# Turning y of three chunks on VectorE and in transfers of 128-byte pieces instead of on TensorE

## The chip, the core and the metric

The kernel runs on one core of a Trainium2 chip. The core has TensorE (PE; its weight loads are listed apart as PEld), VectorE (DVE), ScalarE (ACT), GpSimd (POOL) and SyncE (SP), which here issues every transfer between HBM and the on-chip memory (SBUF). Each of them works through its own instructions strictly in order. PSUM is the small memory that TensorE writes. Sixteen DMA engines carry the transfers. The metric is the time of one execution on the device, in microseconds (us).

## The reference, cut to what matters

```python
x  = A_x                                             # 2048 tokens x 512
xn = layernorm(x)
s  = attention(xn, A_wqkv) @ A_wo                    # 32 heads of 16, a window of 256 keys
y  = layernorm(xn)                                   # what this change is about
h  = gelu(y @ B_w1 + B_b1)                           # 1792 columns
g  = silu(h @ B_w2 + B_b2)
return x + s * g
```

A matmul contracts over the 128 partitions of its operands. y is made with tokens on the partitions (a layernorm is a sum along a row), and `y @ B_w1` needs it with the 512 model columns on the partitions: four blocks `kt` of 128 columns by 512 tokens. Getting from the one to the other is what "turning" means below. Products are taken in a split form: a tile is cut into a rounded high part (by ACT) and the rest (by DVE), and three matmuls stand for one (`PASSES`, line 67; `split`, line 69).

## The kernel before, in words

The first 430 us or so are attention, which the change does not touch. Then comes the MLP, over four chunks of 512 tokens. Chunk 0's y was turned earlier, during attention (`y_turn`).

**The loops (lines 1060 to 1155).** For c = 0 and 1 a loop runs over i = 0 to 14. At each i, `activate` (line 1070) takes the hidden product `h` of column block f through Gelu on ACT into `g` and cuts it into `gh` (ACT) and `gl` (DVE); `project` (line 919) adds the block before into four `acc` banks with twelve matmuls; `hidden` (line 1065) makes the product `h` of the block after next with twelve matmuls, into one of two banks. For c = 0 nearly all hidden products were made during attention, so the loop there is a row of `project` blocks. Then `end_chunk` (line 929) adds b2 (DVE), takes Silu (ACT, `gated`), and for each of four token blocks i calls `between(i)`, makes `s`, the attention's output projection (twelve matmuls, two banks in turn), multiplies it into `gated` (DVE), adds x (POOL, `xo`) and stores.

**Chunks 2 and 3** are computed together after these loops by a recursive scheme with seven products, whose inputs are y of chunk 2, y of chunk 3 and sums and differences of their blocks (`t1` to `t4`). They are prepared inside the loop of c = 1.

**Where y is turned, before.** Chunk 1: `between(0)` and `between(2)` of c = 0 call `y_transpose` (line 642): for each block, four TensorE transposes into a PSUM bank `yt`, then `split` into `mlp["yy"]`, the input of the hidden products of c = 1. Chunk 2: `first_y` (line 996) at i = 3 and 4 of c = 1. Chunk 3: `second_y` (line 1002) at i = 8 and 10, with two steps `more` and `most` called at i = 9, 11 and 12 (line 1089). `transposed` (line 986) issues the four transposes of a block. y of chunks 2 and 3 is loaded from x and normalised twice (`steps2`, line 1051): statistics on DVE, a power on POOL, the scaling on ACT.

**What sets the order.** On PE, DVE, ACT and POOL the order is that of the program text, so everything behind a waiting instruction waits too. SP's order in this part is set by a scheduler (line 855); once set it is also strict. SP's transfers take turns on eight completion counters, so one transfer is issued only when the eighth before it has landed.

**Other transfers that matter here.** `load_o` (line 893) fetches attention output `or` and a broadcast reciprocal `w` (from `rden_d`); both are 256 KB in eight groups of sixteen rows. The y tiles of chunks 1 to 3 share four buffers (`yp`, line 867): a tile of the next chunk can be loaded only when the last reader of the old one is done. Small tiles, `g`, `or` and `xo` among them, share five buffers (`t2`, line 58).

Of the kernel before, what the change touches and what calls it, by code (L numbers as in the profile page):

```python
# [9 lines left out]
F32 = mybir.dt.float32  # L10
# [8 lines left out]
P = 128  # L19
NCH = S // 512  # L20
NKB = S // P
KT = D // P
# [28 lines left out]
def mixer_kernel(ctx, tc, x, wqk, wv, wo, w1, b1, w2, b2, out):  # L51


    nc = SimpleNamespace(**{name: Ordered(tc, name) for name in ("tensor", "vector", "scalar", "gpsimd", "sync")})
# [3 lines left out]
    t2 = ctx.enter_context(tc.tile_pool(name="t2", bufs=5))  # L58
    small = ctx.enter_context(tc.tile_pool(name="small", bufs=3))
    dram = ctx.enter_context(tc.tile_pool(name="dram", bufs=1, space=bass.MemoryType.DRAM))  # L60
# [8 lines left out]
    def split(dst_hi, dst_lo, src, eng=None):  # L69

        (eng or nc.scalar.copy)(dst_hi, src)
        nc.vector.tensor_sub(dst_lo, src, dst_hi.bitcast(F32))
# [87 lines left out]
    def run(steps):  # L160
        for step in steps:
            step()
# [13 lines left out]
    def open_slot(i):  # L176
# [9 lines left out]
    w_d = {"w1": dram.tile([P, NF * 512], F32, name="w1_d"), "w2": dram.tile([P, NF * 512], F32, name="w2_d"),  # L186
           "wo": dram.tile([P, 4 * 512], F32, name="wo_d")}
    g_d = dram.tile([NF, P, 512], F32, name="g_d")
    mT_d = dram.tile([NQ, NCH, 32, P], F32, name="mT_d")


# [31 lines left out]
    ident = const.tile([P, P], F32, name="ident")  # L223
# [360 lines left out]
    mlp = {}  # L584
# [54 lines left out]
    def y_steps(a, b):  # L639
        run(mlp["ln"][a:b])  # L640

    def y_transpose(c, kt, ps=None):
        ts = mlp["y"]
        if ps is None:
            ps = ps_yt.tile([P, 512], F32, tag="b", name=f"yt_{c}_{kt}")
        for i in range(4):
            nc.tensor.transpose(ps[:, P * i: P * (i + 1)], ts[i][:, P * kt: P * (kt + 1)], ident)
        split(mlp["yy"][0][kt], mlp["yy"][1][kt], ps)

    def hidden_mm(ps, f, k):  # L650
        kt, (a, b) = k // 3, PASSES[k % 3]
        nc.tensor.matmul(ps, w1_part(a, f)[:, P * kt: P * (kt + 1)], mlp["yy"][b][kt],
                         start=(k == 0), stop=(k == 3 * KT - 1))
# [209 lines left out]
    ps_yt = ctx.enter_context(tc.tile_pool(name="ps_yt", bufs=2, space=PSUM))  # L863
# [9 lines left out]
    for f in range(6, NF, 2):  # L873
        t = gp.tile([P, 2, 512], F32, tag="ohl", name=f"hr_{f}", bufs=4)
# [7 lines left out]
    def load_y(c):  # L882
        if c > 1:
            return load_x(c, ((mlp["yp"], "y"),), "y")
        return [load(mlp["yp"], "y", xn_d[4 * c + i], f"y_{c}_{i}") for i in range(4)]

    def fetch_sums():
        den = t2.tile([P, 512], F32, tag="t2", name="den")
        for g in range(4):
            nc.sync.dma_start(den[32 * g: 32 * g + 32], oT_d[g, :, DH].rearrange("a (c t) -> a c t", c=NCH))  # L890
        return den
# [84 lines left out]
    kept = {}  # L976
# [6 lines left out]
        first = 256 * (j % (2 if j < 4 else 4))  # L983
        return at[:, first: first + 256 * n]

    def transposed(c, kt):
        ps = ps_yt.tile([P, 512], F32, tag="b", name=f"yt_{c}_{kt}")
        for i in range(4):
            nc.tensor.transpose(ps[:, P * i: P * (i + 1)], mlp["y"][i][:, P * kt: P * (kt + 1)], ident)
        return ps  # L990

    def put(name, kt, src):

        split(inputs(name, kt, 0), inputs(name, kt, 1), src)

    def first_y(kt):

        ps = transposed(2, kt)
        nc.scalar.copy(kept[kt // 2][:, kt % 2], ps)
        put("21" if kt > 1 else "11", kt % 2, ps)  # L1000

    def second_y(kt):

        t1, t4 = kept[0][:, kt], kept[1][:, kt]
        t3, t2_ = (t2.tile([P, 512], F32, tag="t2", name=f"yt{k}_{kt}") for k in (3, 2))
        ps = transposed(3, kt)
        nc.vector.tensor_sub(t1, ps, t1)
        nc.scalar.copy(t3, ps)
        ps = transposed(3, kt + 2)
        nc.vector.tensor_sub(t2_, ps, t1)  # L1010
        nc.vector.tensor_sub(t3, ps, t3)

        def more():
            put("22", kt, ps)
            nc.vector.tensor_sub(t4, t4, t2_)
            put("t1", kt, t1)
            put("t3", kt, t3)

        def most():
            put("t2", kt, t2_)  # L1020
            put("t4", kt, t4)
        return more, most

# [36 lines left out]
    for c in range(2):  # L1060
        accs = open_accs(c)
        gs, os_, hs, wanted = {}, [], {}, []
        made = ready if c == 0 else {}

        def hidden(f):
            hs[f] = ps_st.tile([P, 512], F32, tag="b", name=f"h_{c}_{f}")
            for k in range(3 * KT):
                hidden_mm(hs[f], f, k)

        def activate(f):  # L1070
            if f in made and f in soon:
                gs[f] = made[f]
                return
            src = made[f] if f in made else hs.pop(f)
            g = src if f in made and f < 2 else t2.tile([P, 512], F32, tag="t2", name=f"g_{c}_{f}")
            nc.scalar.activation(g, src, AF.Gelu_apprx_tanh, bias=b1s[:, f: f + 1])
            gs[f] = split_g(c, f, g, nc.scalar.copy)

        order = [2, 3, 0, 1, 4, 5, *range(6, NF)] if c == 0 else [*range(NF)]
        if c:  # L1080
            hidden(0)
            hidden(1)
        o_from, o_late = (0, 0) if c else (8, 1)
        for i in range(NF + 1):
            if i < NF:
                activate(order[i])
            if c and i in (1, 2, 6, 7):
                y_steps(6, 10)
            if c and i in (9, 11):
                rest[0]()  # L1090
            if c and i in (9, 12):
                rest[1]()
            if c and i == 14:
                kept["w"] = bigp.tile([P, 768], F32R, tag="wb1", name="wsh")
                combine_w(0)
            if c == 0:
                for kind, f in late_w[LATE[i]: LATE[i + 1]]:
                    settle(kind, f, nc.scalar.copy, nc.vector)
            if i >= 1:
                project(accs, [(order[i - 1], gs.pop(order[i - 1]))], order[0], order[-1])  # L1100
            if i + 2 < NF and order[i + 2] not in made and order[i + 2] > 1:
                hidden(order[i + 2])
            if c == 0:
                if i == 2:
                    den = fetch_sums()
                if 4 <= i < 8:
                    nc.vector.reciprocal(den[:, P * (i - 4): P * (i - 3)], den[:, P * (i - 4): P * (i - 3)])
                    if i == 7:
                        nc.sync.dma_start(rden_d.rearrange("g a (c t) -> (g a c) t", c=NCH), den)
                if i == 4:  # L1110
                    mlp["y"] = load_y(1)
                if i == 6:
                    mlp["ln"] = layernorm(mlp["y"], "C1", False)
                for back, (a, b) in enumerate(((0, 2), (2, 4), (4, 5), (5, 6), (6, 8), (8, 10))):
                    if i == 6 + min(back, 5):
                        y_steps(a, b)
            else:
                steps2(i)
                if i == 3:
                    kept[0] = gated[:, 2:4]  # L1120
                    first_y(0)
                    first_y(1)
                if i == 4:
                    kept[1] = bigp.tile([P, 2, 512], F32, tag="wb1", name="y2_21")
                    first_y(2)
                    first_y(3)
                    mlp["y"] = load_y(3)
                if i in (8, 10):
                    rest = second_y(i // 10)
                if i == 12:  # L1130
                    fetch_pair(0)
            k = i - o_from
            if 0 <= k - 2 - o_late < 4:
                os_.append(split_o(c, k - 2 - o_late, wanted[k - 2 - o_late][0]))
            if 0 <= k - 1 - o_late < 4:
                nc.vector.tensor_mul(wanted[k - 1 - o_late][0], *wanted[k - 1 - o_late])
            if 0 <= k < 4:
                wanted.append(load_o(c, k))
            if c and i in (0, 1, 5, 6):
                y_steps(5, 6)  # L1140
        if c == 0:
            gated = bigp.tile([P, 4, 512], F32, tag="wa", name="gated")

        def between(i):
            if c == 0 and i in (0, 2):
                y_transpose(1, i)
                y_transpose(1, i + 1)
                if i == 2:
                    mlp["y"] = load_y(2)
            if c == 1 and i in (1, 2):  # L1150
                split_w(0, 2 * i - 2)
                split_w(0, 2 * i - 1)
        end_chunk(c, accs, os_, between)
        if c == 0:
            steps2(-1)
# [148 lines left out]
```

## Time and profile before

| what | us |
|---|---|
| median of 3 runs | 750.75 (750.43 to 750.79) |
| the profiled execution | 750.88 |
| its span, first to last instruction | 749.2 |
| PE busy in the span | 733.9 |
| DVE, ACT, POOL busy | 511.7, 441.1, 299.3 |
| the granted clock of TensorE, mean of the span | 1.0 |

All numbers below come from one profiled execution. Its span is 1.7 us shorter than its own time; the rest lies around the first and the last instruction. Because helper functions issue all instructions, every row names line 43, and rows are told apart by the tiles they write and read (`out<-in`). A bracket at the end of a row of the timeline says how long the engine had been idle and what ended it. In the view of stretches each engine has its busy time and in brackets its count of instructions; then come the granted clock, the mean busy share of the sixteen DMA engines, and GB/s.

### The profile page before, as it was taken

The page shows a single profiled execution, that of the slowest core. Times are in us where ns is not written, and L with a number is a line of the kernel's source. Part 1 is how long each engine was busy: PE and PEld are TensorE (multiplying, and loading weights), DVE is VectorE, ACT ScalarE, POOL GpSimd, SP SyncE. Part 2 cuts the span into 40 slices and gives each one's busy share as a digit, 9 for nine tenths or more (in the row PEclk, how much of TensorE's full clock was granted, in tenths as well). Part 3 has the DMA queues.
Part 4 walks back from the last instruction along what each step waited for, and adds up shares of the span by engine and source line. Part 5 has one row for each costly group of instructions (what it writes and reads, how often), then busy time and mean ns, then how long its engine had stood idle before and what let it go on. Part 6 is the DMA issues. An engine that isn't in the chain of part 4 may idle for free.

```text
span 749.2 us, 18758 instructions
## 1 busy us (share of the span) xinstructions
PE 733.9 (98%) x7408; PEld 590.4 (79%) x7408; DVE 511.7 (68%) x781; ACT 441.1 (59%) x746; POOL 299.3 (40%) x644
## 2 busy tenths in 40 slices
PE   8999999999999999999999999999999999999997
PEld 7886777777778888777776788888888888888886
DVE  7886777877766778887872648763576765676743
ACT  7757767867667676778877745444463744442001
POOL 7413757767666555767877600120102000001102
PEclk9999999999999999999999999999999999999999
DMA  8633356766555535647724482542012232253611
GB/s 288 191 74 78 84 133 149 201 168 183 152 142 145 144 90 142 162 111 190 200 86 148 133 286 94 165 151 82 31 45 102 93 100 72 70 174 123 222 45 56
DMA packets 56951, 99.40 MB, mean 133 GB/s; under 512 B 11104, under 2 KB 11360, under 8 KB 56864
## 3 DMA queue, kind: packets, MB, share of 16 engines
q1 hardware_dynamic: 56864, 98.21, 45.7%
q8 instruction: 58, 0.95, 0.5%
q14 instruction: 29, 0.24, 0.1%
HBM read 51.39 MB, written 29.62 MB: 108 GB/s over the span
## 4 chain that ended last, share of the span: by engine, by line
PE 89%; ACT 5%; DVE 2%; POOL 2%; issue 1%; DMA 1%; SPq 0%; DVEq 0%; ACTq 0%; POOLq 0%
PE acc L43 20%; PE fb L43 18%; PE zo L43 11%; PE stb L43 9%; PE p L43 9%; PE s L43 6%; PE h L43 6%; PE xy L43 5%; ACT pt L43 4%; PE pv L43 3%; POOL pt L43 1%; DVE xy L43 1%; PE yt L43 1%; DMA x<-in_x_dram 1%; DVE mt L43 0%
## 5 line engine op out<-in xcount | busy, mean ns | idle before, releaser
L43 POOL TENSOR_SCALAR_AFFINE_SELECT pt<-pt 128x256 f32<-128x256 f32 x480 | 193.8, 428 | 132.9 <-ACT pt L43 131.7
L43 ACT ACTIVATE pt<-stb 128x768 f32<-128x768 f32 (+1 forms) x244 | 188.8, 774 | 62.4 <-PE stb L43 54.8
L43 DVE TENSOR_REDUCE mt<-xy 128x4 f32<-128x1024 f32 (+1 forms) x128 | 152.6, 1192 | 4.4
L43 DVE COPY_PREDICATED xy<-upper,zo 128x512 f32<-128x512 int32 x112 | 77.8, 695 | 70.6 <-PE xy L43 63.1
L43 POOL TENSOR_TENSOR xo<-xo,gated 128x512 f32<-128x512 f32 x15 | 20.3, 1358 | 216.8 <-DVE gated L43 192.9
L43 PE MATMUL fb<-xnT,wqb 64*128 64x512 f32 (+1 forms) x684 | 104.8, 397 | 0.3
L43 PE MATMUL zo<-pt,vt 128*17 128x128 f32 x2880 | 103.7, 275 | 0.3 <-POOL pt L43 0.3
L43 PE MATMUL stb<-qk 64*128 64x384 f32 (+1 forms) x488 | 97.2, 393 | 6.2 <-ACT pt L43 4.1
L43 PE MATMUL acc<-w,gh 128*128 128x512 f32 x320 | 98.9, 390 | 0.0
L43 PEld LDWEIGHTS stb<-qk 64*128 64x128 f32 x488 | 45.8, 183 | 51.6 <-ACT pt L43 46.6
L43 PEld LDWEIGHTS zo<-pt,vt 128*17 128x17 f32 x2880 | 67.5, 97 | 15.6 <-issue 6.3
L43 PEld LDWEIGHTS fb<-xnT,wqb 64*128 64x128 f32 (+1 forms) x684 | 64.7, 185 | 11.0 <-DVE pjr L43 1.4
L43 PEld LDWEIGHTS acc<-w,gh 128*128 128x128 f32 x320 | 59.8, 188 | 12.3
L43 PE MATMUL acc<-w,gl 128*128 128x512 f32 x160 | 62.4, 390 | 0.0
L43 PE MATMUL xy<-qk 64*128 64x256 f32 (+2 forms) x536 | 58.4, 291 | 0.2 <-DVE mt L43 0.2
L43 PEld LDWEIGHTS xy<-qk 64*128 64x128 f32 x536 | 46.7, 185 | 6.7 <-issue 3.1
L43 ACT COPY oraw<-zo 128x128 f32<-128x128 f32 x128 | 34.2, 267 | 29.2 <-PE zo L43 28.9
L43 ACT ACTIVATE gated<-acc 128x512 f32<-128x512 f32 x16 | 8.7, 596 | 65.6 <-DVE acc L43 65.6
L43 PE MATMUL s<-wos,ohl 128*128 128x512 f32 (+1 forms) x204 | 44.7, 378 | 0.0
L43 PEld LDWEIGHTS s<-wos,ohl 128*128 128x128 f32 x204 | 36.7, 188 | 7.2 <-DVE gated L43 0.2
L43 PEld LDWEIGHTS zo<-qk 64*128 64x128 f32 x448 | 38.5, 185 | 4.4 <-issue 1.4
L43 ACT COPY p<-p 128x512 f32<-128x512 f32 x21 | 12.3, 586 | 49.7 <-PE p L43 42.3
(195 smaller groups left out, 1241.5 us busy)
## 6 DMA issues: line engine op xcount, KB each, us to landing
qk<-sh SPq DMA_DIRECT2D x128, 128.0 KB
qk<-pjr SPq DMA_DIRECT2D x64, 128.0 KB
oT_d<-oraw SPq DMA_DIRECT2D x32, 256.0 KB
w_d<-in_w_dram SPq DMA_DIRECT2D x14, 512.0 KB
x<-in_x_dram SPq DMA_DIRECT2D x16, 256.0 KB
or<-oT_d SPq DMA_DIRECT2D x16, 256.0 KB
w<-rden_d SPq DMA_DIRECT2D x16, 256.0 KB
xo<-in_x_dram SPq DMA_DIRECT2D x16, 256.0 KB
```

The source lines that it names most:

```text
L43: r = issue(*args, **kwargs)
```

## The change

For chunks 1, 2 and 3 the TensorE transposes go away. `turn_y` has DVE transpose a tile of y (128 tokens x 512) in place, each square of 32 x 32 on its own, and stores the tile to a scratch tensor `z_d` in HBM. `fetch_y` then puts one block `kt` in place with four transfers of 64 KB: each writes 32 partitions, sixteen pieces of 128 bytes per partition, 512 pieces in all. So a chunk has four DVE transposes, four stores and sixteen fetches.

Chunk 1 is turned at i = 11 and 12 of c = 0 and fetched at i = 13 straight into the low halves of `mlp["yy"]`; `settle_y`, in `between(0)` and `between(2)`, makes the split there. Chunk 2 is turned at i = 3 of c = 1, fetched at i = 4 and split by `first_y` at i = 5 and 6. Chunk 3 is turned at i = 8, fetched by halves at i = 8 and 10, used by `second_y` at i = 9 and 11, with `more` and `most` at i = 10, 12 and 13. The loads of the next chunk's y move with the fetches.

```diff
+    z_d = dram.tile([NCH, 4, P, 512], F32, name="z_d")
...
-    def y_transpose(c, kt, ps=None):
-        ts = mlp["y"]
-        if ps is None:
-            ps = ps_yt.tile([P, 512], F32, tag="b", name=f"yt_{c}_{kt}")
-        for i in range(4):
-            nc.tensor.transpose(ps[:, P * i: P * (i + 1)], ts[i][:, P * kt: P * (kt + 1)], ident)
-        split(mlp["yy"][0][kt], mlp["yy"][1][kt], ps)
...
+    def turn_y(c, i):
+
+        y = mlp["y"][i]
+        nc.vector.transpose(y, y)
+        nc.sync.dma_start(z_d[c, i], y)
+
+    def fetch_y(c, kt, dst):
+
+        for k in range(4):
+            at = z_d[c, 0, 0, 128 * kt + 32 * k: 128 * kt + 32 * k + 32]
+            nc.sync.dma_start(dst[32 * k: 32 * k + 32].rearrange("p (t j) -> p t j", j=32),
+                              bass.AP(tensor=at.tensor, offset=at.offset, ap=[[512, 32], [32 * 512, 16], [1, 32]]))
+
+    def settle_y(kt):
+
+        hi, lo = mlp["yy"][0][kt], mlp["yy"][1][kt]
+        split(hi, lo, lo.bitcast(F32))
...
-    def transposed(c, kt):
-        ps = ps_yt.tile([P, 512], F32, tag="b", name=f"yt_{c}_{kt}")
-        for i in range(4):
-            nc.tensor.transpose(ps[:, P * i: P * (i + 1)], mlp["y"][i][:, P * kt: P * (kt + 1)], ident)
-        return ps
...
     def first_y(kt):
 
-        ps = transposed(2, kt)
-        nc.scalar.copy(kept[kt // 2][:, kt % 2], ps)
-        put("21" if kt > 1 else "11", kt % 2, ps)
+        put("21" if kt > 1 else "11", kt % 2, kept[kt // 2][:, kt % 2])
+
+    def fetch_second(kt):
+
+        kept["y3"] = [t2.tile([P, 512], F32, tag="t2", name=f"y3_{k}") for k in (kt, kt + 2)]
+        for k, t in enumerate(kept["y3"]):
+            fetch_y(3, kt + 2 * k, t)
 
     def second_y(kt):
 
         t1, t4 = kept[0][:, kt], kept[1][:, kt]
-        t3, t2_ = (t2.tile([P, 512], F32, tag="t2", name=f"yt{k}_{kt}") for k in (3, 2))
-        ps = transposed(3, kt)
-        nc.vector.tensor_sub(t1, ps, t1)
-        nc.scalar.copy(t3, ps)
-        ps = transposed(3, kt + 2)
-        nc.vector.tensor_sub(t2_, ps, t1)
-        nc.vector.tensor_sub(t3, ps, t3)
+        one, two = kept["y3"]
+        nc.vector.tensor_sub(t1, one, t1)
+        nc.vector.tensor_sub(one, two, one)
 
         def more():
-            put("22", kt, ps)
-            nc.vector.tensor_sub(t4, t4, t2_)
+            put("22", kt, two)
             put("t1", kt, t1)
-            put("t3", kt, t3)
+            put("t3", kt, one)
 
         def most():
-            put("t2", kt, t2_)
+            nc.vector.tensor_sub(two, two, t1)
+            put("t2", kt, two)
+            nc.vector.tensor_sub(t4, t4, two)
             put("t4", kt, t4)
         return more, most
...
-            if c and i in (9, 11):
+            if c and i in (10, 12):
                 rest[0]()
-            if c and i in (9, 12):
+            if c and i in (10, 13):
                 rest[1]()
...
+                if i in (11, 12):
+                    turn_y(1, 2 * i - 22)
+                    turn_y(1, 2 * i - 21)
+                if i == 13:
+                    for kt in range(KT):
+                        fetch_y(1, kt, mlp["yy"][1][kt].bitcast(F32))
+                    mlp["y"] = load_y(2)
             else:
                 steps2(i)
                 if i == 3:
+                    for k in range(4):
+                        turn_y(2, k)
+                if i == 4:
                     kept[0] = gated[:, 2:4]
-                    first_y(0)
-                    first_y(1)
-                if i == 4:
                     kept[1] = bigp.tile([P, 2, 512], F32, tag="wb1", name="y2_21")
-                    first_y(2)
-                    first_y(3)
+                    for kt in range(KT):
+                        fetch_y(2, kt, kept[kt // 2][:, kt % 2])
                     mlp["y"] = load_y(3)
-                if i in (8, 10):
-                    rest = second_y(i // 10)
+                if i in (5, 6):
+                    first_y(2 * i - 10)
+                    first_y(2 * i - 9)
+                if i == 8:
+                    for k in range(4):
+                        turn_y(3, k)
+                    fetch_second(0)
+                if i in (9, 11):
+                    rest = second_y(i // 11)
+                if i == 10:
+                    fetch_second(1)
...
         def between(i):
             if c == 0 and i in (0, 2):
-                y_transpose(1, i)
-                y_transpose(1, i + 1)
-                if i == 2:
-                    mlp["y"] = load_y(2)
+                settle_y(i)
+                settle_y(i + 1)
```

## The prediction

> **What bounds the kernel now.** First the page, then the chain of work that ended last, cut to the end of chunk 0 and the loop of c = 1.
>
> ```profile
> span 749.2 us, 18758 instructions
> PE 733.9 (98%) x7408; PEld 590.4 (79%) x7408; DVE 511.7 (68%) x781; ACT 441.1 (59%) x746; POOL 299.3 (40%) x644
> ```
>
> ```profile
> 446.16 30.12 PE acc L43 x132
> 476.27 0.87 PE yt L43 x8
> 477.15 5.46 PE s L43 x24
> 482.61 0.87 PE yt L43 x8
> 483.48 5.68 PE s L43 x24
> 489.16 8.16 PE h L43 x36
> ...
> 510.92 2.72 PE h L43 x12
> ...
> 554.48 0.88 PE yt L43 x8
> ```
>
> TensorE is never idle here: each piece begins where the one before ends. Twelve matmuls take 2.72 us. The transposes stand on the chain in six groups of eight, 0.87 us each, two at the end of chunk 0 and four in the loop of c = 1. What is taken off PE is won, and what makes PE wait is lost.
>
> What will supply y instead is SP's queue, so its timeline comes next, with the first load of the kernel and a row from attention (64 KB and more into 32 partitions, three-level pattern).
>
> ```profile
> 0.79 1.81 SPq L43 DMA_DIRECT2D x<-in_x_dram  x4
> ...
> 191.68 2.54 SPq L43 DMA_DIRECT2D qk<-sh  x4
> ...
> 457.91 0.32 SPq L43 DMA_DIRECT2D rden_d<-den  x1
> 458.28 0.62 SPq L43 DMA_DIRECT2D or<-oT_d  x1
> 459.88 1.20 SPq L43 DMA_DIRECT2D w<-rden_d  x2
> 461.13 0.57 SPq L43 DMA_DIRECT2D or<-oT_d  x1
> 461.75 1.48 SPq L43 DMA_DIRECT2D w<-rden_d  x2
> 463.90 1.08 SPq L43 DMA_DIRECT2D or<-oT_d  x1
> 466.69 3.76 SPq L43 DMA_DIRECT2D w<-rden_d  x2
> ```
>
> ```profile
> 3.57 0.69 DVE L43 BATCH_NORM_STATS2 bnA<-x 128x6 f32<-128x512 f32 x1 [0.68 <-DMA x<-in_x_dram]
> ...
> 467.18 1.00 DVE L43 TENSOR_SCALAR y<-y,mvC,rsC 128x512 f32<-128x512 f32 x2
> 469.76 0.68 DVE L43 TENSOR_TENSOR gl<-g,gh 128x512 fp32r<-128x512 f32 x1
> 472.03 0.69 DVE L43 TENSOR_TENSOR gl<-g,gh 128x512 fp32r<-128x512 f32 x1
> 475.28 0.69 DVE L43 TENSOR_TENSOR or<-or,w 128x512 f32<-128x512 f32 x1 [1.50 <-DMA or<-oT_d]
> ...
> 507.39 0.69 DVE L43 TENSOR_TENSOR gl<-g,gh 128x512 fp32r<-128x512 f32 x1 [1.97 <-ACT gh L43]
> ```
>
> The `or` issued at 463.90 lands only at 475.28, 11.4 us later. A quiet load lands 2.8 us after issue (0.79 to 3.57) and a quiet store within 2.0 (rden_d at 457.91, read from 459.88). So the transfers are backed up exactly where chunk 1's y becomes ready (468.2). The view of stretches shows it: half the capacity of the DMA engines is taken, as it would be with eight of sixteen always busy.
>
> ```profile
> 464.00:470.00 6.00, 6.00 (x29) 4.95 (x28) 4.79 (x10) 2.70 (x4) 0.00 (x0) 1.00 0.48 145
> ```
>
> **Part 1: what PE gains.** 48 transposes go: 6 x 0.87 = 5.2 us, 1.7 of it at the end of chunk 0 and 3.5 in the loop of c = 1. ACT's and DVE's copies out of `yt` are replaced by copies of the fetched tiles, about one for one. POOL gets nothing.
>
> **Part 2: DVE transposes, chunk 1.** No transpose of 512 columns is in the trace. The rows of groups give bounds.
>
> ```profile
> L43 ACT ACTIVATE y<-y,shiftC,rsC 128x512 f32<-128x512 f32 x12 | 8.8, 807 | 8.8 <-DVE shiftC L43 8.8
> L43 DVE TENSOR_TENSOR xnT<-yt,xnT 128x512 fp32r<-128x512 f32 x12 | 8.1, 688 | 10.2 <-ACT xnT L43 10.1
> L43 ACT CAST xnT<-yt 128x512 fp32r<-128x512 f32 x12 | 7.1, 605 | 1.5 <-PE yt L43 1.2 <-PE h L43 0.3
> L43 DVE STREAM_TRANSPOSE mT<-mh 128x32 f32<-128x32 f32 x32 | 6.5, 202 | 0.8 <-POOL mh L43 0.7
> L43 POOL TENSOR_TENSOR rsC<-veC,mhalf 128x4 f32<-128x4 f32 x5 | 5.8, 1169 | 70.6 <-DVE veC L43 70.6
> L43 DVE TENSOR_SCALAR veC<-mvC 128x4 f32<-128x4 f32 x5 | 0.8, 167 | 0.1
> ```
>
> 32 columns take 202 ns and 4 columns of another operation 167, at most 1.25 ns a column: at most 0.8 us for 512; below, 0.2. I take 0.7, the nearest row of that width (688), started 0.6 apart, as an engine's rows in a run overlap a little. On DVE's queue two of them stand before the `gl` of 469.76 and all four before that of 472.03, which thus end at 471.65 and 475.1. PE's last two `project` blocks begin at 470.8 and 473.5 and need them 0.46 later: waits of 0.4 and 0.7, together 1.1 us. s then starts at 477.4 and its first two blocks end at 482.85.
>
> **Part 3: chunk 1's stores and fetches.** The first store stands on SP behind the `w` of 466.69, and is issued when the first transpose is done, at 468.9. Seven transfers of 256 KB from 458.28 on took until 475.28: less 2.0 of latency 2.1 each. The `w` thus lands at 477.4 and the store, with half as many pieces on each of the eight loaded engines, at about 478.2. The load of y_2_0, next in the queue, takes the first tile's buffer, so SP stands until 478.2; stores three and four, done on DVE by 473.2, are queued behind it. They leave at about 479, and the fetches wait for the last one: 481.2 if it lands as in quiet, 483 with what is queued before it; I take 482.0.
>
> Issue: four transfers in 2.54 us, 0.64 each, with the same kind of pattern. Landing: taken 2.3, between 2.0 and 2.8. The eighth fetch leaves at 486.5 and lands at 488.8, the sixteenth at 491.6 and 493.9. Behind the eighth come a cast (0.6) and a subtraction (0.7), and, behind that on DVE, the product with `gated` (0.7) that frees the bank of the third s block: 490.8. PE is idle from 482.85 to 490.8, 7.95 us. ACT waits at the casts with nothing due. The second half of the fetches (493.9 + 1.3) is ready before s ends at 496.3. POOL's adds, `xo` and the stores out are late but wanted by nobody soon.
>
> **The clock.** An idle stretch this long has a second price. The start of PE's timeline, and stretches at the start and the end; the last column but two is the granted clock.
>
> ```profile
> 1.29 4.17 PE L43 MATMUL zo<-upper 128*128 128x128 f32 x22 [1.29 <-DVE zo L43]
> ```
>
> ```profile
> 2.00:3.00 1.00, 1.00 (x7) 1.00 (x7) 0.90 (x2) 0.99 (x2) 1.00 (x1) 1.00 0.81 256
> 4.00:5.00 1.00, 1.00 (x10) 1.00 (x9) 0.93 (x4) 0.83 (x1) 0.71 (x2) 1.00 0.85 168
> ...
> 744.00:746.00 2.00, 0.56 (x5) 0.35 (x3) 1.26 (x4) 0.00 (x0) 0.00 (x0) 1.00 0.34 131
> 748.50:749.10 0.60, 0.00 (x0) 0.00 (x0) 0.00 (x0) 0.00 (x0) 0.00 (x0) 0.50 0.00 0
> ```
>
> PE's last matmul ends at 744.56; by 748.5 the clock is at 0.50. The small matmuls that start at 1.29 go at 7 per us, from about 4 on at 10. So 7.95 idle us should end at half clock, and as PE came up after about 3 us of work, half of that is lost: 1.5 us (0 if the fall does not come; at most 2, as 7 against 10 per us is less than a half). [...] h starts at 497.8 instead of 489.16: +8.6 net.
>
> **Part 4: chunk 2** (times from the start of h, before 489.16). `gl` ends at +18.9; transposes and stores follow it, the last store lands at +23.4. The fetches leave from +23.5 every 0.64. The last tile of y_3 is queued behind them: leaves +33.7, lands +36.5. Statistics (1.1), power (1.2), the shift and two operations queued before it (0.8) give ACT's scaling at +39.6; it, two casts and one Gelu take until +44.3, when the hidden bank for f = 9 is free. PE gets there after sixteen blocks, +43.5: a wait of 0.8. `gl` of f = 6, behind the same statistics, is ready at +40.4, needed at +41.2.
>
> **Part 5: chunk 3.** The transposes end at +52.5, the last store lands at +54.6, eight fetches at +61.5. `second_y`, `more` and `most` alternate ACT and DVE, eleven steps of 0.5 to 0.7 in a chain, 6.3 us, before ACT reaches the Gelu of f = 11: done at +68.5. PE wants that bank after 24 blocks and the 0.8: +66.1. A wait of 2.4. The last eight fetches land while this goes on. The loop of c = 1: 3.2 of waits less 3.5 of transposes, -0.3.
>
> **Sum.** 8.6 - 0.3 = +8.3. The profiled execution took 750.88, which is 749.2 of span and 1.7 around it, 0.13 above the median of the runs: 750.9 + 8.3 = 759.2; I say 759.
>
> **The price that decides: a fetch.** Pieces of 128 bytes are seen once, 128 of them in a store (the transfers in 63.96 to 64.40 us):
>
> ```profile
> DMA packets 132, 0.02 MB, mean 37 GB/s; under 512 B 132, under 2 KB 132, under 8 KB 132
> ...
> q1 hardware_dynamic: 132, 0.02, 23.8%
> ```
>
> 23.8% of sixteen engines over 0.44 us are 12.7 ns a piece: 512 pieces spread on all sixteen need 0.41 us, less than the issue. At the rate of that transfer as it stands, 37 GB/s, 64 KB need 1.77 us. I take 0.64 by the issue, and keep 0.45 (the first loads, 1.81 for four) and 1.77 as ends. About forty fetch steps lie in series over the three chunks (16, 16, 8).
>
> **Rivals.**
> 1. The pieces, not the issues, set the pace. For it: nothing here reads 128-byte pieces from HBM. Against it: 12.7 ns. Halfway, 1.2 us a fetch, adds 40 x 0.56 = 22: 781; at 1.77 it is 804. Chance 0.2. [...]
> 2. The first store is not held by the backlog, as a store might go past reads. Then only the counter of the `w` of 466.69, free at 477.4, holds the loads ahead of the fetches: the eighth lands at 484.2, PE waits 3.4 and keeps its clock: 753. Against it: the 11.4 us of the `or`. Chance 0.12.
> 3. Faster: the fetches land before they are wanted in all three chunks. It decides at 480.9 for the eighth of chunk 1 (PE free at 482.85 less 2.0), so the first must leave by 474.1. Price: -5.2 + 1.1, 746.8. For it: the DMA engines are half idle, and after 490 the queue is not backed up. Against it: the `w` and its counter. Chance 0.06.
>
> My forecast has 0.5, with 754 to 767 for itself; the rest, 0.12, are waits that I priced too low, above it.
>
> **Numbers.** About 0.2% is what a measurement of this kernel can tell from no change. Faster 0.06 is rival 3; same 0.03 is the edge of rivals 2 and 3; slower 0.91. Range 752.5 to 782: from rival 2 to rival 1's halfway price.
>
> **What would show it.** PE: no `yt`; one gap of about 8 us at the third s block of chunk 0, ended by DVE; the clock at 0.5 after it; two shorter gaps at h in the loop of c = 1, ended by ACT. SP: y_2_0's load held by the first store; sixteen fetches 0.64 apart. Wrong if the stores leave at 469 to 473 and land by 476, or if fetches come over 1 us apart.

## The result, and the profile after

The changed kernel takes 758.16 us (757.54 to 758.63 in four runs), the kernel before 750.77 beside it: 1.0098 times as long, 95% interval 1.0082 to 1.0114. The profiled execution took 758.06, with a span of 756.3. The page of the changed kernel, its span and busy time:

```profile
span 756.3 us, 18805 instructions
PE 732.9 (97%) x7360; PEld 587.3 (78%) x7360; DVE 517.6 (68%) x793; ACT 438.4 (58%) x740; POOL 298.7 (39%) x644
```

48 matmuls fewer, 1.0 us less of PE's busy time (some of it at a slower clock), and 7.1 us more of span. The chain of work that ended last in the changed kernel, cut to the end of chunk 0 and to what PE does in the loop of c = 1:

```profile
485.71 0.63 ACT yh L43
486.37 0.69 DVE xnT L43
487.06 0.61 DVE gated L43
487.71 8.34 PE s L43 x24
496.05 8.16 PE h L43 x36
...
541.24 3.02 PE h L43 x12
...
565.13 3.02 PE h L43 x12
...
576.31 10.88 PE s L43 x48
```

The same row of the chain of the kernel before, for the end of the loop:

```profile
568.97 10.88 PE s L43 x48
```

Two differences hold all of it. h starts at 496.05 instead of 489.16: 6.9 us for the end of chunk 0. From there to the s of chunk 1 it is 80.26 us instead of 79.81: 0.45 more. After that the two kernels run alike. The timeline of TensorE, only the rows with idle time ahead:

```profile
471.55 0.50 PE L43 MATMUL acc<-w,gl 128*128 128x512 f32 x1 [0.45 <-DVE gl L43]
...
475.00 0.50 PE L43 MATMUL acc<-w,gl 128*128 128x512 f32 x1 [0.43 <-DVE gl L43]
...
487.71 8.34 PE L43 MATMUL s<-wos,ohl 128*128 128x512 f32 x24 [4.71 <-DVE gated L43]
...
541.24 0.50 PE L43 MATMUL h<-yh,xnT 128*128 128x512 f32 x1 [1.41 <-ACT g L43]
...
565.13 0.50 PE L43 MATMUL h<-yh,xnT 128*128 128x512 f32 x1 [1.83 <-ACT g L43]
```

These are the five waits that the prediction named, ended by the engines that it named. The timeline of SP's queue around the stores and fetches of chunk 1:

```profile
466.55 0.57 SPq L43 DMA_DIRECT2D w<-rden_d  x1
468.69 0.92 SPq L43 DMA_DIRECT2D z_d<-y  x2
470.92 0.60 SPq L43 DMA_DIRECT2D w<-rden_d  x1
475.52 0.33 SPq L43 DMA_DIRECT2D y<-in_x_dram  x1
475.94 0.86 SPq L43 DMA_DIRECT2D z_d<-y  x2
...
479.89 8.78 SPq L43 DMA_DIRECT2D xnT<-z_d  x16
```

The load of y_2_0 takes the first tile's buffer, so it leaves when the first store has landed: 475.52, 6.8 us after that store's issue. Stores three and four follow, and 3.5 us after the last of them the sixteen fetches, 0.53 apart. The view of stretches, with the granted clock in the last column but two, through the gap and behind it:

```profile
484.00:486.00 2.00, 0.00 (x0) 0.00 (x0) 0.69 (x1) 0.87 (x2) 0.00 (x0) 1.00 0.80 126
486.50:493.33 6.83, 5.62 (x13) 4.46 (x14) 3.24 (x6) 2.52 (x3) 1.28 (x1) 0.50 0.85 180
493.50:496.00 2.50, 2.50 (x13) 2.07 (x12) 0.43 (x1) 0.00 (x0) 1.42 (x2) 1.00 0.73 266
```

The clock is at a half for 6.8 us, 5.6 of which PE works.

### The profile page after: what moved, and what is told of

Same layout as the page of the kernel before. It is cut to its first block, busy times and chain, and to the rows that moved or that the text cites. A ratio compares the mean times of both kernels' runs of the same rounds, so it can differ in the third digit from the quotient of the medians.

```text
span 756.3 us, 18805 instructions
## 1 busy us (share of the span) xinstructions
PE 732.9 (97%) x7360; PEld 587.3 (78%) x7360; DVE 517.6 (68%) x793; ACT 438.4 (58%) x740; POOL 298.7 (39%) x644
## 4 chain that ended last, share of the span: by engine, by line
PE 80%; DVE 6%; ACT 5%; DMA 3%; issue 2%; POOL 1%; SPq 1%; DVEq 0%; ACTq 0%; POOLq 0%
PE fb L43 18%; PE acc L43 15%; PE zo L43 11%; PE p L43 9%; PE stb L43 9%; PE s L43 6%; PE xy L43 5%; PE h L43 4%; ACT pt L43 4%; PE pv L43 3%; SPq L43 1%; POOL pt L43 1%; DVE y L43 1%; DVE xy L43 1%; DMA w<-rden_d 1%
## 5 line engine op out<-in xcount | busy, mean ns | idle before, releaser
L43 PE MATMUL s<-wos,ohl 128*128 128x512 f32 (+1 forms) x204 | 47.2, 392 | 4.7 <-DVE gated L43 4.7
L43 PEld LDWEIGHTS s<-wos,ohl 128*128 128x128 f32 x204 | 38.6, 198 | 12.8 <-DVE gated L43 5.1
```

The costliest lines, as they stand in the source:

```text
L43: r = issue(*args, **kwargs)
```

## The experiments

Medians are of the runs of each kernel; the ratio is to the kernel before on the same chip, with its 95% interval.

| run | us | ratio (interval) |
|---|---|---|
| e1 chunk 1 on TensorE | 753.18 | 1.0029 (1.0018 to 1.0041) |
| e2 chunks 2, 3 on TensorE | 757.80 | 1.0096 (1.0077 to 1.0115) |
| e3 filler matmuls | 757.53 | 1.0089 (1.0074 to 1.0104) |
| e4 loads behind | 757.70 | 1.0094 (1.0079 to 1.0109) |
| e5 half the pieces | 754.37 | 1.0050 (1.0032 to 1.0069) |
| e6 chunk 1 early | 755.39 | 1.0059 (1.0044 to 1.0075) |
| e7 chunks 2, 3 reordered, chunk 1 on TensorE | 746.81 | 0.9950 (0.9936 to 0.9964) |
| e8 e6 and the order of e7 | 749.80 | 0.9991 (0.9982 to 0.9999) |
| e9 of e7, the loads only | 747.26 | 0.9958 (0.9943 to 0.9973) |
| e10 of e7, the turn only | 750.08 | 0.9993 (0.9983 to 1.0002) |
| e11 no loads of w | 751.27 | 1.0005 (0.9994 to 1.0015) |
| e12 all three chunks, order of e7 | 754.25 | 1.0045 (1.0028 to 1.0062) |

### Which chunk costs: e1, e2

e1 puts `y_transpose` back for chunk 1; e2 puts the old `first_y` and `second_y` back for chunks 2 and 3.

```diff
 e1
-                if i in (11, 12): turn_y ...; if i == 13: fetch_y(1, ...); load_y(2)
-                settle_y(i); settle_y(i + 1)
+                y_transpose(1, i); y_transpose(1, i + 1); if i == 2: load_y(2)
 e2: the reverse (chunk 1 as in the changed kernel, the rest as before)
```

> Chunk 1 is turned by TensorE as before, chunks 2 and 3 by VectorE and transfers as in the changed kernel. Theory (the price lies in chunk 1: in the trace of the changed kernel h starts 6.9 us later than before, and from there to the first s of chunk 1 80.26 us pass instead of 79.81): the loop of c = 1 alone costs +0.5, so 751.2, between 750.2 and 752.2, with two waits of PE at h of 1.4 and 1.8 us. Rival (the transfers of chunks 2 and 3 are the cost, and chunk 1's delay only moves it): 754 or more.

> Chunk 1 as in the changed kernel, chunks 2 and 3 turned by TensorE as before. Theory (the parts add): 750.8 + 6.9 = 757.7, between 756.7 and 758.5, with one gap of 4 to 5 us at the third s block and a slow stretch behind it. Rival (they do not add; the gap of chunk 1 is covered by something that the loop of c = 1 gives back): below 756.

e2 took the time that was expected, 757.80; its gap at the third s block, 5.72, is above the 4 to 5 expected. e1 is 2.0 above its number, and its seven runs fall into two groups: five with a mean clock of 0.997 took 753.1 to 753.9, two with 0.999 and 1.0 took 751.5 and 751.9. The view of stretches of e1's profiled execution (one of the five), from the start of its wait for f = 11:

```profile
557.32:559.24 1.92, 0.00 (x1) 0.00 (x1) 1.24 (x3) 1.23 (x3) 0.00 (x0) 1.00 0.00 0
559.24:560.33 1.09, 1.09 (x5) 0.91 (x6) 0.54 (x2) 1.09 (x2) 0.00 (x0) 1.00 0.06 15
560.33:563.74 3.41, 3.41 (x10) 2.67 (x9) 3.38 (x7) 2.28 (x5) 0.00 (x0) 0.50 0.29 85
```

PE is idle for 1.92 us, works for 1.1 at full clock, and then the clock goes to a half for 3.41: 1.7 us for a wait of 1.9. The two quicker runs, 751.7, are by their mean clock the loop without that fall. So the split stands: chunk 1 costs about 7, the loop 1 to 2.7, and they add up to more than the 7.4 of the whole. In the changed kernel, where h starts later, the loop costs less: its wait for gl of f = 6 is about 0.1 instead of 0.77, and no fall of the clock follows its wait for f = 11 (granted 1.00 from 565.13 to 580).

### Whether the clock is a price of its own: e3

```diff
                 settle_y(i + 1)
+                if i == 2:
+                    warm = ps_yt.tile([P, 512], F32, tag="b", name="warm")
+                    for k in range(16):
+                        nc.tensor.matmul(warm, os_[0][:, 0, 0:P], wos[:, 0, 0, :], start=(k == 0), stop=(k == 15))
```

> The changed kernel with sixteen matmuls more (3.6 us at 0.227 each), of operands that are long there, into a bank that nobody reads, between the second and the third s block of chunk 0, where PE stood idle for 4.71 us; nothing of the computation is left out. Theory (the idle time let the clock fall to 0.50, and the 24 matmuls behind it took 8.34 us instead of 5.46 for that reason): PE stays busy, the clock stays at 1.0 and 2.7 us come back: 755.5, between 754.9 and 756.2. Rival (the 24 matmuls were slow for another reason, such as the transfers that fill the DMA engines at that time): 758.2, no change.

In the whole time only 0.6 of the 2.7 came back. Where it was aimed it did what was expected; the chain of work that ended last in e3:

```profile
488.22 5.74 PE s L43 x24
493.95 2.73 PE h L43 x12
...
575.48 10.88 PE s L43 x48
```

The 24 matmuls take 5.74 instead of 8.34, so the clock's price was 2.6. Two things ate it. In this execution the transfers of `w` came late ahead of the edit (a wait of 1.35 for gl at 473 instead of 0.45), and the loop, entered 2.1 earlier, took 81.53 instead of 80.26, with a wait for gl of 1.42 at 536.63. Much of the time won at the end of chunk 0 came back here as a wait in the loop, which is late for a cause of its own (see e9).

### Why the stores land late: e4, e11

```diff
 e4
-                    mlp["y"] = load_y(2)          (at i == 13)
+                if i == 2: mlp["y"] = load_y(2)   (in between, behind settle_y)
 e11
-        nc.sync.dma_start(rec, ...rden_d...)
-        return raw, rec
+        return raw, b2s
```

> The changed kernel, but the four loads of chunk 2's y are called for in between(2), as before the change, so that none of them stands on SP between chunk 1's stores. Theory (the third and fourth store were held by the load that waited for the first store, until 475.5, though VectorE was done with them at 473.3): they leave at about 473, the fetches start at about 478 instead of 479.9, the gap is 2.8 us instead of 4.7, too short for the clock to fall (it fell 3.5 us into the gap): 758.2 - 1.9 - 2.7 = 753.6; 756.3 if the clock falls all the same. Rival (the backlog alone sets when the stores land, and not when they are issued): the fetches start at 479.9 as they did, 758.2.

> The changed kernel without the loads of the broadcast reciprocal w (the attention output is multiplied by another tile instead, so the division is left out). It takes away half of the transfers that go over eight engines. Theory (these back up the queue, and the stores of y stand behind them): the first store lands within 3 us of its issue instead of 6.8, the third and fourth land by 476 instead of 479.8, the fetches start by 476 and the gap at the third s block is at most 1 us, without a fall of the clock: 751.5, up to 754.5 with what comes back as waits in the loop of c = 1. Rival (the stores are slow by themselves, or held by the buffers): fetches still from about 480, 757 to 758.

e4 speaks for its rival, e11 for the theory. SP's queue in e4, where no load stands between the stores:

```profile
473.30 0.89 SPq L43 DMA_DIRECT2D z_d<-y  x2
...
481.56 8.54 SPq L43 DMA_DIRECT2D xnT<-z_d  x16
```

And in e11, without the loads of `w`:

```profile
467.81 1.03 SPq L43 DMA_DIRECT2D z_d<-y  x2
469.95 0.33 SPq L43 DMA_DIRECT2D y<-in_x_dram  x1
...
471.26 0.92 SPq L43 DMA_DIRECT2D z_d<-y  x2
...
475.23 9.18 SPq L43 DMA_DIRECT2D xnT<-z_d  x16
```

In e4 the third and fourth store leave 2.6 us earlier than in the changed kernel, and the fetches leave 1.7 later (the first store left 1.1 later in this execution, which may account for that much): what is issued into the backlog lands no sooner. In e11 the first store lands 2.1 us after its issue instead of 6.8, and the fetches leave at 475.23. So the backlog of `or` and `w` sets it, and the load that SP stood at was only where the delay showed. e11's time, 751.27, is the one expected; its gap at the third s block, 1.59, is above the 1 expected, for a reason that comes with e8.

### What a fetch costs: e5

```diff
-                        fetch_y(1, kt, mlp["yy"][1][kt].bitcast(F32))
+                        fetch_y(1, kt, mlp["yy"][1][kt].bitcast(F32), 8)   # 8 of 16 squares a partition
```

> The changed kernel, but each of chunk 1's sixteen fetches brings 256 pieces of 128 bytes instead of 512: only the first 256 tokens of the chunk are put in place, the others keep an older value. Theory (the pace is set by the issue: 0.49 busy and 0.53 from one to the next on SP's queue): the sixteen still take 8.4 to 8.8 us, the gap at the third s block stays at 4.5 to 5 us. Rival (the pieces set it: 512 pieces on sixteen engines at the 13 ns that the busy share of 0.8 gives are 0.42, not far below 0.53): 256 pieces need 0.21, the step falls towards 0.3, the eighth fetch leaves 1.6 us earlier and the gap falls to about 3 us.

```profile
475.38 0.86 SPq L43 DMA_DIRECT2D z_d<-y  x2
476.34 7.92 SPq L43 DMA_DIRECT2D xnT<-z_d  x16
```

On SP's queue sixteen fetches of half the pieces take 7.92 instead of 8.78: 0.50 from one to the next instead of 0.53. The issue sets the pace. The gap, expected at 4.5 to 5, fell to 1.04 all the same, by something not thought of: the first 256 tokens need only the first two stores, so the fetches left at 476.34, 3.5 us earlier, ahead of the landing of stores three and four. What is left of the gap has another cause, shown with e8.

### Chunk 1 in time: e6, e8

e6 moves the load of chunk 1's y, its normalisation, its turn and its fetches three steps of the loop ahead, and has the loads of e4; e8 adds the order of e7.

```diff
-                if i == 4: mlp["y"] = load_y(1)
-                if i == 6: mlp["ln"] = layernorm(mlp["y"], "C1", False)
+                if i == 1: mlp["y"] = load_y(1)
+                if i == 3: mlp["ln"] = layernorm(mlp["y"], "C1", False)
...
-                if i in (11, 12): turn_y ...
-                if i == 13: fetch_y ...
+                if i in (8, 9): turn_y ...
+                if i == 10: fetch_y ...
```

> The changed kernel, but chunk 1's y is loaded, normalised, turned and fetched three steps of the loop (about 8 us) earlier, and chunk 2's loads are called for in between(2); so the fetches leave from about 468 and land by 479. Theory (chunk 1's price is its late stores, and nothing else in the way of turning): no gap at the third s block and no slow clock; h starts at 488.5 (489.2 less 1.7 of transposes, plus up to 1 of waits for gl), and with a loop of c = 1 that costs 0.5 to 1.5 more than before: 750.8, between 749.5 and 752. Rival (sixteen fetches and four stores hurt wherever they stand, since they are in the way of the loads of the attention output that s needs): a wait of several us moves to the first s block or to the last project blocks, 754 or more.

> The last two together: all three chunks turned by VectorE and transfers, chunk 1 three steps earlier, chunk 3's loads ahead of chunk 2's fetches. Theory (what costs is the place of the transfers on SP's queue; the turning itself is worth 5.2 us less small waits): 746, between 745 and 748, faster than both kernels. Rival (it is not only the place): 750 or more, or a new wait that neither of the two alone shows.

Both miss, by 4.6 and 3.8 us, towards their rivals. The timeline of VectorE in e8, its rows for the attention output and for `gated`:

```profile
475.43 0.69 DVE L43 TENSOR_TENSOR or<-or,w 128x512 f32<-128x512 f32 x1 [1.96 <-DMA w<-rden_d]
...
478.65 0.69 DVE L43 TENSOR_TENSOR or<-or,w 128x512 f32<-128x512 f32 x1 [0.86 <-DMA w<-rden_d]
...
480.44 2.75 DVE L43 TENSOR_TENSOR acc<-acc,b2s 128x512 f32<-128x512 f32 x4
...
486.06 1.28 DVE L43 TENSOR_TENSOR gated<-s,gated 128x512 f32<-128x512 f32 x2
```

The stores now stand ahead of `or` and `w` in the same backlog, so `w` is late (1.96 and 0.86 on VectorE), the additions of b2 start at 480.44 instead of 477.71, and a gap of 2.02 is left at the third s block. PE also waits 0.56, 1.14 and 0.51 for gl, the first two where the statistics were moved to. (This execution, 752.08, is the slowest of eleven, with the clock at a half for 3.41 us behind the gap; the median is 749.80.) In e6 the loop of c = 1, in the old order, took 83.12 us in its profiled execution, with waits of 1.10, 1.41 and 1.96 and the clock at a half for 3.41 behind the last.

A second reason holds even where `w` is not late. The timeline of VectorE of the kernel before, between the last `project` block and the third s block:

```profile
477.08 2.76 DVE L43 TENSOR_TENSOR acc<-acc,b2s 128x512 f32<-128x512 f32 x4
...
482.68 1.28 DVE L43 TENSOR_TENSOR gated<-s,gated 128x512 f32<-128x512 f32 x2
```

The first of these products frees the bank at 483.3, and PE of the kernel before starts its third s block at 483.41. Four additions, four Silus, two casts, two subtractions and a product are a chain of 6.3 us. It began 0.8 us after the last `project` block, so it ended 7.1 us behind that block, and what PE had to do meanwhile, two s blocks and four times four transposes, took just as long, 7.2 us. Take the 1.7 us of transposes away, and PE would wait 1.6 for the chain. e5 shows such a wait with no fetch in it. Its timelines of VectorE and TensorE:

```profile
477.59 2.76 DVE L43 TENSOR_TENSOR acc<-acc,b2s 128x512 f32<-128x512 f32 x4
...
483.22 1.28 DVE L43 TENSOR_TENSOR gated<-s,gated 128x512 f32<-128x512 f32 x2
```

```profile
483.96 5.73 PE L43 MATMUL s<-wos,ohl 128*128 128x512 f32 x24 [1.04 <-DVE gated L43]
```

The product comes 5.63 us behind the first addition, as in the kernel before (5.60), so the chain alone made PE wait 1.04. In e11 a fetch added 0.42 to it:

```profile
483.71 5.75 PE L43 MATMUL s<-wos,ohl 128*128 128x512 f32 x24 [1.59 <-DVE gated L43]
```

So 1.0 us or more of the 1.7 came back in these traces. How much it is hangs on when the additions start, and that is not fixed: in the kernel before the last `or` was waited for until 475.28 and the additions start at 477.08; in e8 the last `w` was waited for until 478.65, and they start at 480.44.

### Chunks 2 and 3 in order: e7, e9, e10, e12

```diff
 the loads (e7, e8, e9, e12)
                     for k in range(4): turn_y(2, k)     (at i == 3)
+                    mlp["y"] = load_y(3)
...
-                    mlp["y"] = load_y(3)                (at i == 4, behind fetch_y(2))
 the turn (e7, e8, e10, e12)
-                if i == 8: turn_y(3, 0..3); fetch_second(0)
+                if i == 7: turn_y(3, 0..3)
+                if i == 8: fetch_second(0)
```

e7, e9 and e10 have chunk 1 on TensorE as e1 has; e12 has all three chunks turned the new way.

> Chunk 1 by TensorE as before; chunks 2 and 3 as in the changed kernel, but chunk 3's y is loaded ahead of chunk 2's fetches instead of with its last tile behind them, and turned one step of the loop earlier. Theory (the waits of PE at h come from that last tile, which left 9 us late, and from the chain behind it): the waits of 0.8, 1.4 and 1.9 us and the slow clock behind the last go, 3.5 us of transposes are won: 747.5, between 746.5 and 749. Rival (the waits come from the work itself, sixteen fetches for each chunk and the subtractions in a chain on VectorE and ScalarE): 750.5 or more.

> Chunk 1 by TensorE, chunks 2 and 3 as in the changed kernel, with only chunk 3's loads moved ahead of chunk 2's fetches; chunk 3 is turned where the changed kernel turns it. Theory (each wait of the loop of c = 1 has its own cause): the waits for gl (0.8) and for the bank of f = 9 (1.4 and a slow start of 0.3) go; the one for f = 11 (1.9 and 0.3), which hangs on the turn queued on VectorE behind a gl that PE releases, stays: 746.8 + 2.2 = 749.0, and 750.8 in executions in which the clock falls behind it. Rival (one cause, the late last tile, behind all of them): 746.8.

> Chunk 1 by TensorE, chunks 2 and 3 as in the changed kernel, with only the turn of chunk 3 moved one step of the loop earlier; the last tile of its loads still stands behind chunk 2's fetches. Theory (each wait has its own cause): the wait for f = 11 goes, those for gl (0.8) and for f = 9 (1.4 and 0.3) stay: 746.8 + 2.5 = 749.3. Rival (one cause, the late last tile): all the waits stay, 751.5 to 753.5.

> The changed kernel, chunk 1 included, with both reorderings of chunks 2 and 3 (chunk 3's loads ahead of chunk 2's fetches, its turn one step earlier). Theory (chunk 1 costs the 6.9 us that h starts later, and with no waits left in the loop of c = 1 nothing of it is hidden): 746.8 + 6.9 = 753.7, between 752.5 and 755. Rival (chunk 1's delay is partly taken up by the loop): below 752.

e7 is faster than both kernels: 746.81. Its chain has no wait in the loop:

```profile
488.80 8.16 PE h L43 x36
...
564.96 10.88 PE s L43 x48
```

76.16 us instead of 79.81: the 3.5 us of transposes, and nothing paid for them. e9 decides against the theory of three causes: with the loads moved alone the time is 747.26, and its timeline of TensorE shows none of the three waits. SP's queue in e1 and then in e9:

```profile
519.14 5.03 SPq L43 DMA_DIRECT2D y<-z_d  x8
524.22 0.49 SPq L43 DMA_DIRECT2D y<-in_x_dram  x1
```

```profile
512.31 2.27 SPq L43 DMA_DIRECT2D y<-in_x_dram  x4
514.64 5.48 SPq L43 DMA_DIRECT2D gated<-z_d  x8
```

The last tile of y_3 leaves by 514.6 instead of at 524.22, and with that the waits for gl, for f = 9 and for f = 11 are gone. e10 shows that the last of them also goes by the turn alone, so it needs both the late tile and the late turn. Its time is 750.08, 0.8 above its number, and the other two waits stay in its timeline of TensorE:

```profile
531.67 0.50 PE L43 MATMUL acc<-w,gl 128*128 128x512 f32 x1 [1.02 <-DVE gl L43]
...
535.65 0.50 PE L43 MATMUL h<-yh,xnT 128*128 128x512 f32 x1 [1.42 <-ACT g L43]
```

e12 came out as expected: 754.25, 7.4 above e7, which is what turning chunk 1 this way costs when nothing behind it takes any of it up.

## Why the prediction was right, and where it was not

The forecast of 759 held, 0.8 from the median, by the mechanism that it named; but of the two terms of its sum, 8.6 for the end of chunk 0 was 6.9 and -0.3 for the loop was +0.45. That the sum is nearer than its terms is in part luck: the idle time was put 3.2 too long, the clock's price 1.1 too low and the loop 0.75 too low.

- Part 1, transposes: 5.2 us taken off PE. Right for the loop, 3.5 predicted and 3.65 shorter in e7. Wrong for most of the 1.7 at the end of chunk 0: "what is taken off PE is won" fails there, because a chain on VectorE and ScalarE was nearly as long, and 1.0 (e5) or more comes back as a wait. The sum did not rest on it, as it took the third s block from the fetches; rival 3's price did.
- Part 2, transposes on VectorE, taken as 0.7: 0.68. The group in the changed kernel:

```profile
L43 DVE STREAM_TRANSPOSE y<-y 128x512 f32<-128x512 f32 x12 | 7.6, 681 | 0.0
```

  The two waits are 0.45 and 0.43 instead of 0.4 and 0.7; s starts at 477.40, as predicted.
- Part 3, idle 7.95: 4.71. Its mechanism stands (store behind the backlog, load behind the store, stores behind the load, fetches behind the stores), three sizes were off. The first store landed at 475.5, not 478.2: the backlog was put 2.7 too long. The fetches left at 479.9, not 482.0. And they went 0.53 apart, not 0.64, with a landing 2.1 after issue instead of 2.3, together 1.0 by the eighth.
- The clock, 1.5: 2.6 by e3. It came back not after 3 us of work but 5.6 us after PE resumed (487.71 to 493.33), for a reason that no run shows.
- Part 4, a wait of 0.8 for f = 9: 1.41, and 0.3 more for the first matmuls behind it (3.02 for twelve instead of 2.72). The last tile left 34.0 after the start of h (33.7 predicted) and ScalarE's last step came 1 later than worked out. The slack of 0.8 for gl of f = 6 was not there: about 0.1 of wait here, 0.77 in e1.
- Part 5, 2.4 for f = 11: 1.83 and 0.3. Its chain is in the trace as written, with eight fetches landed 62.0 after the start of h (61.5 predicted). But it was taken for a cost of its own, and it is not: e9 shows that it goes when the last tile of Part 4 comes in time.
- Rival 1, pieces that set the pace: out, by 0.53 a fetch and by e5. A piece took 13 ns on its engine in these fetches (512 pieces at a busy share of 0.80 over 0.53 us), as in the stores of 128-byte pieces of the kernel before (12.7), of which there are 32 and not one. 64 KB in 0.53 us is 124 GB/s, far above the 37 that the prediction kept as an end.
- Rival 2, the first store not held: out, 6.8 us against 2.1 in e11. That PE keeps its clock through a wait of 3.4, as its price has it, no run shows: in e1 the fall came 3.0 us after the start of a wait of 1.92, in e2 2.1 us into the gap.
- Rival 3, everything in time: not reached by moving chunk 1 ahead (e6, e8), since the stores then hold up `w`, and by Part 1's chain its price was 1.0 to 1.6 too good.

## What to carry to other kernels

Before work is taken off the bounding engine, look whether another chain ends at nearly the same moment: here four groups of transposes were worth their time, and of the other two 1.0 us or more of 1.7 came back as a wait. One load queued behind a burst of small transfers cost 5.9 us here (e1 less e9), while the burst itself cost next to nothing (the loop of e9 has no wait). Moving one call by a few lines turned a loss of 0.3% into a gain of 0.4%. A store issued 2.6 us earlier into the backed-up queue landed no sooner (e4); what helped was to take away what stood in the queue ahead of it (e11).

## What the runs showed of the hardware that was not expected

The granted clock fell to 0.50 behind waits much shorter than the 7.95 us for which the prediction priced it, and the time at a half did not grow with the wait. The gaps of TensorE with a fall in them or behind them, from its timelines and the views of stretches (us):

| run | the gap | from its start to the fall | at a half |
|---|---|---|---|
| e1, f = 11 | 1.92 | 3.0 | 3.41 |
| e6, f = 11 | 1.96 | 3.1 | 3.41 |
| e8, third s block | 2.02 | 3.5 | 3.41 |
| e11, f = 11 | 2.35 | 3.5 | 3.41 |
| the changed kernel, third s block | 4.71 | 3.5 | 6.83 |
| e4, third s block | 5.10 | 5.3 | 3.41 |
| e2, third s block | 5.72 | 2.1 | 6.83 |
| e12, third s block | 6.34 | 5.3 | 6.83 |

In e8 the fall came 1.5 us after PE had gone back to work. In e5 the ten matmuls behind a gap of 2.81 took 4.14 us, where twelve take 2.72 at full clock. What sets the moment of the fall and the time at a half, these runs do not show. The stretches in e4:

```profile
484.13:489.23 5.10, 0.00 (x1) 0.00 (x0) 2.04 (x4) 1.24 (x2) 0.00 (x0) 1.00 0.79 124
489.42:492.83 3.41, 3.41 (x9) 2.64 (x9) 2.50 (x3) 1.82 (x3) 2.40 (x2) 0.50 0.62 151
```

A gap of 5.1 us at full clock, and the half clock only from 0.2 us after it. In e1 the fall came behind a wait of 1.92 us and cost 1.7 more: the same kernel takes 753.4 with that fall and, as its mean clock tells, 751.7 without it.
